# A Fourier-and-gate kernel on one core: the first set of Strassen products reordered, a shared operand left unsplit

## The chip, the cores and the metric

One core of a Trainium2 chip. The metric is the device time of one execution in microseconds; the time of a kernel is the median of several runs. The engines are TensorE (PE), VectorE (DVE), ScalarE (ACT), GpSimd (POOL) and SyncE (SP); SP and POOL issue the transfers, each from a queue of its own, in order.

## The reference

With S = 2048 rows, D = 640 columns and F = 1536 hidden units, all in float32:

```
xn = layernorm(x)                              # rows of 640
a  = xn @ dft_hid_re.T ;  b = xn @ dft_hid_im.T
s  = dft_seq_re @ a - dft_seq_im @ b           # over the 2048 rows
f  = (silu(xn @ w_gate) * (xn @ w_up)) @ w_down
out = x + s * silu(f)
```

The kernel takes the sequence transform first (the DFT matrix over rows times xn, `seq`), then the hidden transform (`hid`), then the gate and up products (`gate_up`) and the down product (`down`).

## The kernel before, in words

**Products.** A float32 product is made of three matmuls in a rounded format: each operand is split into a high part (ScalarE copies it rounded, L192) and a low part (VectorE subtracts, L197 or L199), and `mm3` (L213 to L215) takes high*high, high*low and low*high. A matmul is 128x128 by 128x512.

**Strassen.** `seq(k)` runs four times (two halves of the output rows j, real and imaginary ri). Each time a 1024-row by 2048-column quarter pair of the DFT matrix is cut in four blocks a11, a12, a21, a22 and multiplied by xn's blocks with seven products p1 to p7 over the first 512 columns of xn. The last 128 columns need no Strassen: they are "direct" products that ride beside others into bank 6 or 7, d1 and d2 being xn's upper and lower rows of those columns. D1 = d1*a11 + d2*a12 rides beside p1 and p2. D2 = d1*a21 + d2*a22 is made by a phase of its own, "d" (operand a21 against d1), and by the first pass of p4 (a22 against d2). A product runs in four groups g = 0 to 3, each of two tiles kk of 128 rows; a group of p5 before is 12 matmuls (two banks), a group of d 6, a group of p1 or p2 with its direct product 18.

**The order of the work** is made by a planner. `Plan` counts TensorE's steps at MM = 0.226 us a matmul; each other operation is given a lead (`prod`: so many us ahead of the step that needs it) or an `after` (`post`), and all are sorted by the resulting time and issued in that order, each engine's queue in order. `LEAD` (L541) holds the leads of the first set by hand. Tiles live in two arenas, "hl" for split operands (95 KB a partition) and "raw" for all else (111 KB); `place` and `fit` choose each tile's place from the times at which it is used, so a later tile can have to wait for an earlier one's last reader.

**The opening** (`opening`, first set) runs p1 of k = 0 and, beside it, p1 of k = 1 (it has the same right operand), in eight steps kk of two parts: part 0 into banks b2 and 6, part 1 into banks b1 and b3[0]. Step 0 is unsplit and counts 24 x 0.226 = 5.42 us, each later one 18 matmuls, and the whole 33.90 us. Behind it, sums of part 1 are copied out by two evictions (L241, planned 1 us after the end) to s1 and d1, kept for k = 1. SP loads x tiles 0 to 7 and a11 of both parts for it, x tiles of 128 rows by L412 and parts of the DFT matrix by L684, L686 and L575.

**Behind the opening**, for k = 0: phase d: `d(g)` loads a21 (R[g], 512 KB), splits it, and lets POOL add a22 onto R[g] in memory (`accumulate`, L580, a transfer that adds; it must wait until the split has read R[g]). Then p5, whose left operand is R[g] = a21 + a22, in the order of groups 0, 2, 3, 1, into banks b3; when a group's operand is split, POOL adds a11 onto R[g] for p6. Then p2 with a12, for which x tiles 8 to 15 are loaded (8 and 9 by SP, the others by POOL), normalized (small steps on POOL, L442 to L449) and split. Then p6, p3, p7, p4. For k = 1 to 3 the order is p1 (not for k = 1), d, p2, p5, p6, p3, p7, p4. Sums of xn's blocks that p5, p6, p4 need (nt1, t2, nt4) are made once by `new` (L478) in "raw" and kept through all four sets.

**Gate, up and down.** `gate_up(j)` takes 12 steps f of 54 matmuls; `gate_weights` loads 640 KB (L911) 16 us ahead of each step, forms sums on VectorE (L918) and splits them in four parts. The down product is a Strassen product of the same kind (`strassen`): p1, d, p2, p5 and so on. Its weight operands are prepared during the gate steps of j = 0 by `down_operands`, one name of `d_names` at a time in two slots of each of ten steps f, stored to DRAM split (L533) and loaded from there (L1021).

Of the kernel before, what the change touches and what calls it, by code (L numbers as in the profile page):

```python
# [7 lines left out]
F32 = mybir.dt.float32  # L8
# [14 lines left out]
MM = 0.226  # L23
HL_KB, RAW_KB = 95, 111


class Plan:
# [10 lines left out]
    def buf(self, name, arena, n):  # L38

        for key in ((name, "h"), (name, "l")) if arena == "hl" else (name,):  # L40
            self.size[key] = (arena, n if arena == "raw" else n // 2)
        return name
# [95 lines left out]
def tile_fnet_swiglu(  # L138
# [23 lines left out]
    hl_arena = one.tile([P, HL_KB * 256], F32R, name="hl")  # L162
    raw_arena = one.tile([P, RAW_KB * 256], F32, name="raw")
    ps = psum.tile([P, 8, TC], F32, name="ps")
    mv = one.tile([P, NS, 2], F32, name="mv")
# [7 lines left out]
    def raw(name, a=0, n=None):  # L173
        o = where[name]
        return raw_arena[:, o + a:o + (pl.size[name][1] if n is None else a + n)]

    def hl(name, i, a=0, n=None):

        key = name, "hl"[i]
        o = where[key]  # L180
        return hl_arena[:, o + a:o + (pl.size[key][1] if n is None else a + n)]

# [68 lines left out]
    def strassen(tag, groups, get, top, dop, result, end=False):  # L251
# [72 lines left out]

        def a21(g):
            X[g] = get(21, g)
            return operand("d", g, X[g])

        def a12(g):
# [3 lines left out]
        def s_1(g):  # L333
            V[g] = get(22, g)
            name = pl.buf(("W", tag, g), "raw", n[g])
            W[g] = (name, 0, (name, 0))
            (xn_, xa, xk), (vn, va, vk) = X[g], V[g]
            pl.prod(12, lambda: nc.vector.tensor_tensor(
                raw(name), raw(xn_, xa, n[g]), raw(vn, va, n[g]), op=ALU.add), [xk, vk], [(name, 0)])
            return operand("p5", g, W[g])  # L340
# [15 lines left out]
        evict(s1, b2)  # L356
        phase("d", None, a21, (2, 1))
        phase("p2", b1, a12, (1, 2))
        result(11, b1, s1, ALU.subtract)
        result("d1", (dbank[1],), None, None)  # L360
        phase("p5", b3, s_1)
        n5 = copies("n5")
# [14 lines left out]
        if not end:  # L377
            run("p4", ops["p4"], None, None, None, (2, 2))
            result("d2", (dbank[2],), None, None)
            run("p4", ops["p4"], b2, w, wk)  # L380
            result(21, b2, None, None)
            return
        dw, dkeys = dop(2)

# [82 lines left out]
    def right(p, g, lead):  # L467


        def quad(h, c, w=256):  # L470
            k = 8 * h + 4 * g
            return (lambda a=0, n=4: xn_tiles(k + a, n, 256 * c, w)), [(xn, i, c) for i in range(k, k + 4)]

        def new(what, a, b, op):
            if (what, g) not in sums:
                name = pl.buf((what, g), "raw", 1024)
                view = lambda a=0, n=4: raw(name).rearrange("p (a b) -> p a b", b=256)[:, a:a + n]
                pl.prod(lead, lambda: nc.vector.tensor_tensor(view(), a[0](), b[0](), op=op), [*a[1], *b[1]], [(name, 0)])  # L478
                sums[what, g] = view, [(name, 0)]
            return sums[what, g]  # L480

        if p == "p1":
            return quad(0, 0)
        if p == "p2":
            return quad(1, 0)
        if p == "p3":
            return quad(1, 1)
        if p == "p5":
            return new("nt1", quad(0, 0), quad(0, 1), ALU.subtract)
        if p == "p6":  # L490
            return new("t2", quad(1, 1), sums["nt1", g], ALU.add)
        if p == "p4":
            return new("nt4", quad(1, 0), sums["t2", g], ALU.subtract)
        if p == "p7":
            a, b = quad(0, 1), quad(1, 1)
            if ("nt3", g) not in sums:
                pl.prod(lead, lambda: nc.vector.tensor_tensor(a[0](), a[0](), b[0](), op=ALU.subtract), b[1], a[1])
                sums["nt3", g] = a
            return a
        return quad(int(p[1]) - 1, 2, P)  # L500


    d_names = ("p1", "p2", "d1", "d2", "p3", "p5", "p6", "p7", "p4")
    d_dram = {(p, g): dram.tile([P, 768 if p[0] == "d" else 1536], F32, name=f"d_{p}_{g}") for g in range(2) for p in d_names}

    def down_operands():

        for g in range(2):
# [10 lines left out]
            for p in d_names:  # L519
                b11, b12, b21, b22 = (quad(*q) for q in ((0, 0), (0, 1), (1, 0), (1, 1)))  # L520
                made = {"p5": (b11, b12, ALU.subtract), "p6": (b11, b22, ALU.add),
                        "p7": (b12, b22, ALU.subtract), "p4": (b21, b11, ALU.subtract)}
                if p in made:
# [22 lines left out]

# [8 lines left out]
    def seq(k):  # L555
# [54 lines left out]

        def run(*parts, order=None):

# [4 lines left out]
            start = pl.now  # L617
            for i, g in order or [(0, g) for g in range(4)]:
                p, left, banks, direct = parts[i]
                rights = ([p] if banks else []) + ([f"d{direct[1]}"] if direct else [])  # L620
                per = 3 * (len(banks) + (direct is not None))
                at = pl.now
                s = left(g)
                for kk in (2 * g, 2 * g + 1):
                    pl.now = at + kk % 2 * per * MM
                    for r in rights:
                        few = 4 if not fresh or r not in ("p1", "d1", "p2", "d2") else 2 if g > 2 or r[1] == "2" else 1
                        if (r, kk) not in top:
                            right_operand(r, kk // few, few)
                pl.now = at + 2 * per * MM  # L630
                todo.append((p, g, banks, direct, rights, s))
# [29 lines left out]
        def copy(what, b):  # L661
            name = pl.buf((what, k), "raw", 2 * TC)
            evict(name, b, after=3)
            return name
# [3 lines left out]
        def opening():  # L668
# [42 lines left out]
            for kk in range(8):  # L711
                for i, banks, db in part:
                    c = left[i, kk // 2]
# [13 lines left out]
            ahead["d1"] = pl.buf(("d1", 1), "raw", TC)  # L727
            evict(ahead["s1"], b1, after=1)
            evict(ahead["d1"], (b3[0],), after=1)

# [3 lines left out]

        def p5(g):
            s = operand("p5", g, R[g])
            if fresh:
                accumulate(R[g], 11, g, LEAD["p5", g][1] - 0.1)
            return s

        def d(g):
            R[g] = load(21, g, 26 if fresh else 18)
            s = operand("d", g, R[g])
            accumulate(R[g], 22, g, LEAD["d"][1] - 0.1 if fresh else 7.5)
            return s

        def p2(g):
            if fresh:
                for kk in (8 + 2 * g, 9 + 2 * g):
                    load_x(kk, (32, 27.5, 25.4, 29.4)[g], nc.gpsimd if g else nc.sync)  # L750
                layer_norm(8 + 2 * g, 2, *LEAD["xn", 4 + g], nc.gpsimd)
            return operand("p2", g, load(12, g, 11 if fresh else 17))

# [9 lines left out]
        def p3(g):  # L763
            add(R[g], load(12, g, 17), 12)
            return operand("p3", g, R[g])
# [10 lines left out]
        s1 = ahead["s1"] if shared else copy("s1", b2)  # L776
        run(("d", d, (), (2, 1)))
        if not fresh:
            product_2()
        run(("p5", p5, b3, None), order=((0, 0), (0, 2), (0, 3), (0, 1)) if fresh else None)  # L780
        n5 = copy("n5", b3)
# [15 lines left out]
        def p4(g):  # L797
            last.append(operand("p4", g, load(22, g, 17)))
            return last[-1]

        run(("p4", p4, (), (2, 2)))
        result("d2", (dbank[2],), None, None)
# [104 lines left out]
    def gate_weights(j, f):  # L907
        names = [pl.buf(("W", j, f, i), "hl", 2 * n) for i, n in enumerate((512, 640, 640, 384))]
        w = pl.buf(("wraw", j, f), "raw", 1280)
# [22 lines left out]
    def gate_up(j):  # L932
# [5 lines left out]
        for f in range(NF):  # L938
# [44 lines left out]
            pl.post(lambda g1=g1: nc.scalar.activation(raw(g1), raw(g1), AF.Silu, scale=-1.0), [(g1, 0)], [(g1, 0)])  # L983
            if j == 0 and f and f != NF - 1:
                next(spare, None)
# [22 lines left out]
            tail.append(last)  # L1008
            if j == 0 and f and f != NF - 1:
                next(spare, None)  # L1010
# [71 lines left out]

    where.update(pl.place({"hl": HL_KB * 256, "raw": RAW_KB * 256}))

# [4 lines left out]
    started = False  # L1089
    for t, _, fn, names, _ in pl.ops:  # L1090
        if t >= 0 and not started:
# [43 lines left out]
```

## Time and profile before

| | us |
|---|---|
| median of 3 runs | 992.88 (992.24 to 993.19) |
| the profiled execution, its time | 993.8 |
| the profiled execution, its span (first to last instruction) | 991.7 |
| TensorE busy | 979.3 |
| VectorE busy | 717.2 |
| ScalarE busy | 497.8 |
| POOL busy | 106.4 |
| mean granted clock of TensorE | 0.995 of full |

The span leaves out 2.1 us of the profiled execution's time. All times inside the run are microseconds from the span's start. TensorE's matmuls overlap, so its duration per matmul (0.39 us in the timeline) is longer than the distance of two starts (0.227 us); the distance is what adds up.

### The profile page before, as it was taken

The page shows a single profiled execution, that of the slowest core. Times are in us where ns is not written, and L with a number is a line of the kernel's source. Part 1 is how long each engine was busy: PE and PEld are TensorE (multiplying, and loading weights), DVE is VectorE, ACT ScalarE, POOL GpSimd, SP SyncE. Part 2 cuts the span into 40 slices and gives each one's busy share as a digit, 9 for nine tenths or more (in the row PEclk, how much of TensorE's full clock was granted, in tenths as well). Part 3 has the DMA queues.
Part 4 walks back from the last instruction along what each step waited for, and adds up shares of the span by engine and source line. Part 5 has one row for each costly group of instructions (what it writes and reads, how often), then busy time and mean ns, then how long its engine had stood idle before and what let it go on. Part 6 is the DMA issues. An engine that isn't in the chain of part 4 may idle for free.

```text
span 991.7 us, 11754 instructions
## 1 busy us (share of the span) xinstructions
PE 979.3 (99%) x4300; PEld 804.7 (81%) x4300; DVE 717.2 (72%) x942; ACT 497.8 (50%) x716; POOL 106.4 (11%) x175
## 2 busy tenths in 40 slices
PE   9989999999999999999999999999999999999998
PEld 5778888788888888888888888888888888888886
DVE  6889867965875595377678787687568666666685
ACT  5585652755455554424655555444334544445342
POOL 0380111011101010000111110000010100000000
PEclk9989999999999999999999999999999999999999
DMA  9788687575757493842645344679860211105683
GB/s 337 208 210 227 223 217 180 171 237 135 180 191 222 108 264 116 288 163 107 250 191 181 138 165 164 211 264 354 293 230 28 89 45 53 54 27 191 219 290 127
DMA packets 72185, 182.18 MB, mean 184 GB/s; under 512 B 6528, under 2 KB 22144, under 8 KB 72128
## 3 DMA queue, kind: packets, MB, share of 16 engines
q1 hardware_dynamic: 57792, 127.81, 38.0%
q0 software_dynamic: 14336, 53.63, 19.6%
q8 instruction: 33, 0.54, 0.2%
q14 instruction: 24, 0.20, 0.1%
HBM read 147.85 MB, written 33.57 MB: 183 GB/s over the span
## 4 chain that ended last, share of the span: by engine, by line
PE 91%; DMA 3%; DVE 2%; ACT 2%; issue 1%; SPq 0%; POOL 0%; DVEq 0%; ACTq 0%
PE ps L214 30%; PE ps L213 30%; PE ps L215 30%; DMA raw<-in_cs 3%; DVE hl L197 1%; ACT hl L192 1%; DMA p_dram<-raw 1%; ACT raw L454 0%; DVE raw L583 0%; DVE bst L421 0%; ACT raw L241 0%; POOL raw L580 0%; DVE raw L246 0%; SPq L686 0%; SPq L412 0%
## 5 line engine op out<-in xcount | busy, mean ns | idle before, releaser
L213 PE MATMUL ps<-hl 128*128 128x512 f32 (+1 forms) x1424 | 554.6, 389 | 5.3 <-ACT raw L241 5.3
L214 PE MATMUL ps<-hl 128*128 128x512 f32 (+1 forms) x1424 | 554.0, 389 | 0.1
L215 PE MATMUL ps<-hl 128*128 128x512 f32 (+1 forms) x1424 | 553.6, 389 | 0.0
L192 ACT ACTIVATE hl<-raw 128x1024 fp32r<-128x1024 f32 (+7 forms) x509 | 374.5, 782 | 284.4 <-PE ps L215 54.1
L197 DVE TENSOR_TENSOR hl<-raw,hl 128x1024 fp32r<-128x1024 f32 (+5 forms) x438 | 394.7, 931 | 121.8 <-ACT hl L192 76.9
L213 PEld LDWEIGHTS ps<-hl 128*128 128x128 f32 x1424 | 268.0, 188 | 62.5 <-ACT raw L241 6.1
L214 PEld LDWEIGHTS ps<-hl 128*128 128x128 f32 x1424 | 267.9, 188 | 56.2 <-DVE hl L197 0.7
L215 PEld LDWEIGHTS ps<-hl 128*128 128x128 f32 x1424 | 267.9, 188 | 55.2
L241 ACT ACTIVATE raw<-ps 128x512 f32<-128x512 f32 (+1 forms) x120 | 78.0, 670 | 106.6 <-PE ps L215 80.9
L246 DVE TENSOR_TENSOR raw<-ps,raw 128x512 f32<-128x512 f32 (+1 forms) x93 | 74.6, 803 | 54.1 <-PE ps L215 52.4
L1005 DVE TENSOR_TENSOR raw<-raw 128x512 f32<-128x512 f32 x24 | 16.6, 692 | 50.1 <-ACT raw L1004 50.0
L918 DVE TENSOR_TENSOR raw<-raw 128x256 f32<-128x256 f32 (+1 forms) x96 | 47.7, 518 | 0.0
L580 POOL DMA_DIRECT2D raw<-in_cs x36 | 32.3, 953 | 140.3 <-DVE raw L583 81.0
L199 DVE SCALAR_TENSOR_TENSOR hl<-raw,hl 128x384 fp32r<-128x384 f32 (+4 forms) x71 | 41.2, 580 | 7.3 <-PE ps L215 2.9
L583 DVE TENSOR_TENSOR raw<-raw 128x1024 f32<-128x1024 f32 x28 | 34.1, 1219 | 10.8 <-DMA raw<-in_cs 10.7
L1067 POOL DMA_DIRECT2D out<-raw x10 | 6.7, 671 | 302.1 <-DMA hl<-d_p 175.1
L657 POOL DMA_DIRECT2D p_dram<-raw x24 | 17.5, 772 | 198.1 <-DVE raw L246 163.4
L871 DVE TENSOR_TENSOR raw<-raw 128x1024 f32<-128x1024 f32 (+1 forms) x24 | 23.9, 1040 | 6.8 <-DMA raw<-in_xt 4.7
L983 ACT ACTIVATE raw<-raw 128x512 f32<-128x512 f32 x24 | 15.2, 632 | 22.1 <-DVE raw L246 22.1
L843 POOL DMA_DIRECT2D y_dram<-raw x20 | 10.8, 546 | 132.5 <-ACT raw L241 132.5
L1004 ACT ACTIVATE raw<-ps 128x512 f32<-128x512 f32 x24 | 14.3, 594 | 21.0 <-PE ps L215 21.0
L533 POOL DMA_DIRECT2D d_p<-hl x28 | 15.1, 541 | 79.7 <-ACT hl L192 65.6
(49 smaller groups left out, 191.6 us busy)
## 6 DMA issues: line engine op xcount, KB each, us to landing
raw<-in_cs SPq DMA_DIRECT2D x82, 512.0 KB, 6.1
hl<-d_p SPq DMA_DIRECT2D x56, 384.0 KB, 4.4
raw<-in_cs POOLq DMA_DIRECT2D x36, 512.0 KB, 8.9
raw<-in_wb SPq DMA_DIRECT2D x24, 640.0 KB, 4.5
d_p<-hl POOLq DMA_DIRECT2D x28, 384.0 KB, 2.9
raw<-p_dram SPq DMA_DIRECT2D x8, 1280.0 KB, 11.1
p_dram<-raw POOLq DMA_DIRECT2D x16, 512.0 KB, 7.5
raw<-in_hd SPq DMA_DIRECT2D x20, 320.0 KB, 8.1
```

Source lines behind the costliest of these rows:

```text
L192: nc.scalar.activation(like(hl(dst, 0, a, n)), src(), AF.Copy, scale=1.0 if scale is None else scale)
L197: nc.vector.tensor_tensor(lo, src(), hi, op=ALU.subtract)
L199: nc.vector.scalar_tensor_tensor(lo, src(), scale, hi, op0=ALU.mult, op1=ALU.subtract)
L213: nc.tensor.matmul(o, w(0), m(0), start=first, stop=False, skip_group_check=True)
L214: nc.tensor.matmul(o, w(0), m(1), start=False, stop=False, skip_group_check=True)
L215: nc.tensor.matmul(o, w(1), m(0), start=False, stop=True, skip_group_check=True)
L241: pl.post(lambda: nc.scalar.activation(wide(raw(dst, a, n)), pair(b), AF.Copy), pkeys(b), [(dst, a)], after)
L246: pl.post(lambda: nc.vector.tensor_tensor(wide(raw(dst, a, n)), pair(b), wide(raw(other)), op=op), [*pkeys(b), (other, 0)], [(dst, a)], after)
L580: pl.prod(lead, lambda: nc.gpsimd.dma_start(wide(raw(name)), source(q, g), accum_op=ALU.add), [], [(name, 0), (name, 1)], 8)
L583: pl.prod(lead, lambda: nc.vector.tensor_tensor(raw(dst), raw(dst), raw(src), op=ALU.add), [(src, 0)], [(dst, 0)])
L871: pl.prod(46 - 6 * q - 2 * i - half, lambda i=i, op=op, part=part, rows=rows, nb=nb: nc.vector.tensor_tensor(part(), part(), raw(rows, i * ...
L918: pl.prod(lead, lambda o=o, a=a, b=b, op=op: nc.vector.tensor_tensor(o(), a(), b(), op=op), [(w, 0)], [(c, lead)])
```

## The change

D2 is now d1*(a21 + a22) + d3*a22 with d3 = d2 - d1. The phase d is gone in all sets and in the down product: its direct product rides beside p5 with p5's own operand, and a21 is split nowhere. d3 is one more sum of xn's blocks (`nt5`) and one more name among the down weights, in whose slots now all twelve steps f of the first gate pass take part. In the first set p5 follows straight on the opening, in the order 0 to 3; a21's loads, a22's accumulates and the x tiles 8 to 15 (all on SP now) have earlier leads; the last opening step takes part 1 first, and the two evictions are planned 1.5 and 1 us ahead of its end instead of 1 us behind. The sums (and s1 of the first set) lie in an area "raw2" of 28 KB, which is closed after its last use and opened again as "hl2" for parts 1 to 3 of the gate weights; "hl" falls to 84 KB and "raw" to 94. Some leads of loads grow by 3 us.

```diff
-HL_KB, RAW_KB = 95, 111
+HL_KB, RAW_KB, TURN_KB = 84, 94, 28
...
-        def a21(g):
-            X[g] = get(21, g)
-            return operand("d", g, X[g])
-
         def s_1(g):
-            V[g] = get(22, g)
+            X[g], V[g] = get(21, g), get(22, g)
...
-        phase("d", None, a21, (2, 1))
         phase("p2", b1, a12, (1, 2))
...
-        phase("p5", b3, s_1)
+        phase("p5", b3, s_1, (2, 1))
...
-            run("p4", ops["p4"], None, None, None, (2, 2))
+            run("p4", ops["p4"], None, None, None, (2, 3))
...
-        def new(what, a, b, op):
+        def new(what, a, b, op, w=256):
             if (what, g) not in sums:
-                name = pl.buf((what, g), "raw", 1024)
+                name = pl.buf((what, g), "raw2", 4 * w)
...
+        if p == "d3":
+            return new("nt5", quad(1, 2, P), quad(0, 2, P), ALU.subtract, P)
...
-    d_names = ("p1", "p2", "d1", "d2", "p3", "p5", "p6", "p7", "p4")
+    d_names = ("p1", "p2", "d1", "d2", "d3", "p3", "p5", "p6", "p7", "p4")
...
-            ("p5", 0): (7.7, 6.7), ("p5", 1): (8.4, 7.4), ("p5", 2): (7.2, 6.2), ("p5", 3): (7.4, 6.4), "p2": (8, 6), "d": (8.7, 8.4)}
+            "Tp2": (0, 6, 4), "Td2": (0, 6, 4), "T": (14, 13, 11), "S": (10, 8), "p5": (7.4, 6.4), "p2": (8, 6)}
...
-            name = pl.buf((what, k), "raw", 2 * TC)
+            name = pl.buf((what, k), "raw2" if fresh and what == "s1" else "raw", 2 * TC)
...
-                for i, banks, db in part:
+                for i, banks, db in part if kk < 7 else part[::-1]:
...
-            evict(ahead["s1"], b1, after=1)
-            evict(ahead["d1"], (b3[0],), after=1)
+            evict(ahead["d1"], (b3[0],), after=-1.5)
+            evict(ahead["s1"], b1, after=-1)
...
         def p5(g):
+            R[g] = load(21, g, 33 + 4 * g if fresh else 26)
+            accumulate(R[g], 22, g, 22 + 2 * g if fresh else 18)
             s = operand("p5", g, R[g])
             if fresh:
-                accumulate(R[g], 11, g, LEAD["p5", g][1] - 0.1)
-            return s
-
-        def d(g):
-            R[g] = load(21, g, 26 if fresh else 18)
-            s = operand("d", g, R[g])
-            accumulate(R[g], 22, g, LEAD["d"][1] - 0.1 if fresh else 7.5)
+                accumulate(R[g], 11, g, LEAD["p5"][1] - 0.1)
             return s
...
-                    load_x(kk, (32, 27.5, 25.4, 29.4)[g], nc.gpsimd if g else nc.sync)
+                    load_x(kk, 40 + 2 * g, nc.sync)
...
-            return operand("p2", g, load(12, g, 11 if fresh else 17))
+            return operand("p2", g, load(12, g, 11 if fresh else 20))
...
-        run(("d", d, (), (2, 1)))
         if not fresh:
             product_2()
-        run(("p5", p5, b3, None), order=((0, 0), (0, 2), (0, 3), (0, 1)) if fresh else None)
+        run(("p5", p5, b3, (2, 1)))
...
-        run(("p4", p4, (), (2, 2)))
+        run(("p4", p4, (), (2, 3)))
...
-        names = [pl.buf(("W", j, f, i), "hl", 2 * n) for i, n in enumerate((512, 640, 640, 384))]
+        names = [pl.buf(("W", j, f, i), "hl2" if i else "hl", 2 * n) for i, n in enumerate((512, 640, 640, 384))]
...
-            if j == 0 and f and f != NF - 1:
+            if j == 0:
                 next(spare, None)
...
-    for t, _, fn, names, _ in pl.ops:
+    first = ExitStack()
+    space["raw2"] = first.enter_context(tc.tile_pool(name="sums", bufs=1)).tile([P, TURN_KB * 256], F32, name="raw2")
+    for i, (t, _, fn, names, _) in enumerate(pl.ops):
+        if i == turn:
+            first.close()
+            space["hl2"] = ctx.enter_context(tc.tile_pool(name="parts", bufs=1, reuse_waits="tile")).tile(
+                [P, TURN_KB * 256], F32R, name="hl2")
```

## Rows read from the trace of the kernel before

**Rows 1.** The page: span, busy time of each engine (share of the span, instructions).
```profile
span 991.7 us, 11754 instructions
...
PE 979.3 (99%) x4300; PEld 804.7 (81%) x4300; DVE 717.2 (72%) x942; ACT 497.8 (50%) x716; POOL 106.4 (11%) x175
```

**Rows 2.** TensorE's waits (us, times, longest): whole run, then 100 to 991 us.
```profile
PE ps L213 <- ACT raw L241: 5.3, 2, 5.0
...
PE ps L213 <- ACT raw L241: 0.2, 1, 0.2
```

**Rows 3.** Windows: length, busy of each engine (x instructions), granted clock, DMA share, GB/s.
```profile
12.48:41.10 28.62, 28.62 (x126) 23.18 (x125) 24.58 (x57) 19.40 (x32) 4.38 (x6) 1.00 0.79 289
...
47.20:52.20 5.00, 0.04 (x1) 0.00 (x0) 2.22 (x5) 2.42 (x4) 4.55 (x10) 0.85 1.07 211
52.20:57.55 5.35, 5.26 (x12) 4.12 (x13) 5.28 (x10) 5.35 (x8) 4.51 (x6) 0.50 1.04 332
```

**Rows 4.** TensorE's timeline around the hole: start, duration, what, [idle before].
```profile
46.85 0.39 PE L215 MATMUL ps<-hl 128*128 128x512 f32 x1
52.28 0.79 PE L213 MATMUL ps<-hl 128*128 128x512 f32 x1 [5.05 <-ACT raw L241]
...
57.55 0.40 PE L213 MATMUL ps<-hl 128*128 128x512 f32 x1
```

**Rows 5.** The chain of waits, 36 to 53 us: start, duration, engine and line.
```profile
39.50 10.25 DMA raw<-in_cs
...
49.78 1.06 ACT hl L192
50.83 1.41 ACT raw L241 x2
```

**Rows 6.** POOL's timeline: the first accumulate.
```profile
36.72 1.06 POOL L580 DMA_DIRECT2D raw<-in_cs  x1 [35.39 <-DVE hl L197]
```

**Rows 7.** SP's timeline, 14 to 23 us, and the landing of its first four L575.
```profile
15.30 3.78 SPq L575 DMA_DIRECT2D raw<-in_cs  x4
19.55 1.12 SPq L412 DMA_DIRECT2D raw<-in_x  x2
...
DMA to landing us min/median/max: 8.9/9.3/9.3
```

**Rows 8.** Accumulates (L580), issue to landing: the first one, then all 12 to 100 us.
```profile
DMA to landing us min/median/max: 5.7/5.7/5.7
...
DMA to landing us min/median/max: 5.7/8.9/14.6
```

**Rows 9.** DMA: windows as in rows 3; then 36 to 60 us in 40 slices, share and GB/s.
```profile
24.00:31.00 7.00, 7.00 (x33) 5.79 (x32) 5.69 (x18) 4.67 (x11) 0.00 (x0) 1.00 1.03 402
31.00:36.70 5.70, 5.70 (x27) 4.72 (x26) 4.63 (x8) 5.67 (x10) 0.00 (x0) 1.00 0.14 57
...
DMA  0000929998997999999999999999999999999995
GB/s 0 0 0 0 123 41 218 212 205 220 316 205 247 316 218 218 198 191 218 218 198 198 212 198 218 212 212 212 205 218 381 427 418 418 410 289 205 218 212 96
```

**Rows 10.** Groups by line and shape: the splits (busy us, mean ns, idle before).
```profile
L197 DVE TENSOR_TENSOR hl<-raw,hl 128x1024 fp32r<-128x1024 f32 x186 | 220.4, 1220 | 61.8 <-ACT hl L192 38.6 <-PE ps L214 11.8 <-PE ps L215 11.3
L192 ACT ACTIVATE hl<-raw 128x1024 fp32r<-128x1024 f32 x190 | 191.8, 1052 | 126.7 <-PE ps L214 37.2 <-PE ps L215 34.1 <-DVE raw L885 14.0
...
L197 DVE TENSOR_TENSOR hl<-raw,hl 128x1536 fp32r<-128x1536 f32 x32 | 55.9, 1754 | 16.3 <-ACT hl L192 12.1 <-PE ps L215 2.4 <-PE ps L214 1.1
...
L192 ACT ACTIVATE hl<-raw 128x1536 fp32r<-128x1536 f32 x32 | 46.9, 1485 | 38.1 <-DVE raw L288 20.6 <-issue 7.3 <-PE ps L215 7.2
L197 DVE TENSOR_TENSOR hl<-raw,hl 128x512 fp32r<-128x512 f32 x62 | 42.6, 687 | 21.3 <-ACT hl L192 9.6 <-PE ps L214 8.1 <-PE ps L215 2.0
```

**Rows 11.** Gate weights: their loads (KB each, us to landing) and first sum.
```profile
raw<-in_wb SPq DMA_DIRECT2D x24, 640.0 KB, 4.5
...
L918 DVE TENSOR_TENSOR raw<-raw 128x640 f32<-128x640 f32 x24 | 19.6, 818 | 0.0
```

More of the change, by code (lines that the diff above doesn't have):

```diff
@@ L38, in buf @@
     def buf(self, name, arena, n):
-        for key in ((name, "h"), (name, "l")) if arena == "hl" else (name,):
-            self.size[key] = (arena, n if arena == "raw" else n // 2)
+        split = arena[:2] == "hl"
+        for key in ((name, "h"), (name, "l")) if split else (name,):
+            self.size[key] = (arena, n // 2 if split else n)
         return name
@@ L163, in tile_fnet_swiglu @@
     raw_arena = one.tile([P, RAW_KB * 256], F32, name="raw")
+    space = {"hl": hl_arena, "raw": raw_arena}
     ps = psum.tile([P, 8, TC], F32, name="ps")
@@ L174, in raw @@
         o = where[name]
-        return raw_arena[:, o + a:o + (pl.size[name][1] if n is None else a + n)]
+        arena, size = pl.size[name]
+        return space[arena][:, o + a:o + (size if n is None else a + n)]
     def hl(name, i, a=0, n=None):
@@ L180, in hl @@
         o = where[key]
-        return hl_arena[:, o + a:o + (pl.size[key][1] if n is None else a + n)]
+        arena, size = pl.size[key]
+        return space[arena][:, o + a:o + (size if n is None else a + n)]
     def split(lead, dst, n, src, reads, a=0, scale=None, sub=0, low_lead=None):
@@ L382, in strassen @@
             return
-        dw, dkeys = dop(2)
+        dw, dkeys = dop(3)
         def alone(bank, weights, keys, first, a=0, n=TC):
@@ L472, in quad @@
             return (lambda a=0, n=4: xn_tiles(k + a, n, 256 * c, w)), [(xn, i, c) for i in range(k, k + 4)]
-        def new(what, a, b, op):
+        def new(what, a, b, op, w=256):
             if (what, g) not in sums:
-                name = pl.buf((what, g), "raw", 1024)
-                view = lambda a=0, n=4: raw(name).rearrange("p (a b) -> p a b", b=256)[:, a:a + n]
+                name = pl.buf((what, g), "raw2", 4 * w)
+                view = lambda a=0, n=4: raw(name).rearrange("p (a b) -> p a b", b=w)[:, a:a + n]
                 pl.prod(lead, lambda: nc.vector.tensor_tensor(view(), a[0](), b[0](), op=op), [*a[1], *b[1]], [(name, 0)])
@@ L521, in down_operands @@
                 made = {"p5": (b11, b12, ALU.subtract), "p6": (b11, b22, ALU.add),
-                        "p7": (b12, b22, ALU.subtract), "p4": (b21, b11, ALU.subtract)}
+                        "p7": (b12, b22, ALU.subtract), "p4": (b21, b11, ALU.subtract),
+                        "d3": (quad(1, 2, P), quad(0, 2, P), ALU.subtract)}
                 if p in made:
@@ L609, in tw, with run @@
             return lambda part: hl(name, part, at + e * P, P)
-        def run(*parts, order=None):
+        def run(part):
             todo = []
             start = pl.now
-            for i, g in order or [(0, g) for g in range(4)]:
-                p, left, banks, direct = parts[i]
+            p, left, banks, direct = part
+            for g in range(4):
                 rights = ([p] if banks else []) + ([f"d{direct[1]}"] if direct else [])
@@ L763, in p3 @@
         def p3(g):
-            add(R[g], load(12, g, 17), 12)
+            add(R[g], load(12, g, 20), 12)
             return operand("p3", g, R[g])
@@ L797, in p4 @@
         def p4(g):
-            last.append(operand("p4", g, load(22, g, 17)))
+            last.append(operand("p4", g, load(22, g, 20)))
             return last[-1]
-        run(("p4", p4, (), (2, 2)))
+        run(("p4", p4, (), (2, 3)))
         result("d2", (dbank[2],), None, None)
@@ L1008, in gate_up @@
             tail.append(last)
-            if j == 0 and f and f != NF - 1:
+            if j == 0:
                 next(spare, None)
@@ L1081, in tile_fnet_swiglu @@
         down(j)
-    where.update(pl.place({"hl": HL_KB * 256, "raw": RAW_KB * 256}))
+    where.update(pl.place({"hl": HL_KB * 256, "raw": RAW_KB * 256, "raw2": TURN_KB * 256, "hl2": TURN_KB * 256}))
+    uses = [{pl.size[n if n in pl.size else (n, "h")][0] for n in names if n in pl.size or (n, "h") in pl.size} | {
+        pl.size[n][0] for n in names if n in pl.size} for _, _, _, names, _ in pl.ops]
+    turn = 1 + max(i for i, u in enumerate(uses) if "raw2" in u)
+    assert not any("hl2" in u for u in uses[:turn])
     nc.gpsimd.memset(sm[:, 5, :8], EPS)
```

1 row of the table LEAD is left out of this document.

## The prediction

> **What bounds the kernel now.** I began with the page's table of busy time [rows 1]: TensorE is busy 979.3 of 991.7 us, so only what happens while it is idle or slow can change the time. The waits of TensorE come next [rows 2]: over the whole run it waited 5.3 us in two places for ScalarE's evictions at L241, and behind 100 us only 0.2 us of that is left. So there is one hole, of 5.0 us. The timeline of TensorE places it [rows 4]: a matmul starts at 46.85, the next at 52.28. The windows around it show the second half of the price [rows 3]: in the opening TensorE ran 126 matmuls in 28.62 us at full granted clock, 0.227 us each; behind the hole, from 52.20 to 57.55, the granted clock is 0.50 (1.2 GHz instead of 2.4) and 12 matmuls take the time of 23. From the start at 46.85 to the start at 57.55 there are 13 matmuls: 10.70 us where 13 x 0.227 = 2.95 are due. **The hole costs 7.75 us in all**: some 5.2 of standing and some 2.55 of slow clock.
>
> Why it is there, by the chain of waits [rows 5]: an accumulate landed at 49.75 after 10.25 us, ScalarE split that operand from 49.78, and only then, from 50.83, ran the evictions for which TensorE waited. Those evictions had their sums since the end of the opening, 6 us earlier; they stood behind the split in ScalarE's queue. By the plan's numbers that is so: the second p5 group (g = 2) is due at 33.90 + 5.42 + 2.71 - 7.2 = 34.83, the evictions at 33.90 + 1 = 34.90. And the accumulate was late because POOL could start the first of them only at 36.72, after 35.39 us of waiting for a VectorE split [rows 6]: a22 is added in place onto a21, and a21's own split had to be read out first. The loads of a21 had been issued at 15.30 and took 8.9 to 9.3 us [rows 7], so the first lay there from about 24.6. Between 31.0 and 36.7 the DMA engines moved 57 GB/s, against 402 before [rows 9]: they stood almost still, waiting for that split.
>
> **The change, part by part.** TensorE's work does not shrink. d1*a21 + d2*a22 becomes d1*(a21+a22) + (d2-d1)*a22: 24 matmuls of d move into p5 and 24 stay in p4, the same number of the same shape. So no term of TensorE's busy time goes.
>
> *Splits.* Gone are 16 splits of 128x1024 in the four sets and 4 of 128x1536 in the down products: ScalarE 16 x 1.052 + 4 x 1.485 = 22.8 us, VectorE 16 x 1.220 + 4 x 1.754 = 26.5 us [rows 10]. Added are 8 splits of 128x512 for d3, 8 x 0.687 = 5.5 us on VectorE and about as much on ScalarE, two sums nt5, by the same row about 1.4 us, and for the down weights two sums, two splits, four stores and eight loads of small tiles, some microseconds over the whole run. All of it lies on engines that TensorE does not wait for behind 100 us [rows 2]: I price it at nothing. If the cover were gone, the two extra steps beside the gate products would cost what VectorE lacks there; it is 72% busy over the run [rows 1].
>
> *The first set.* Accumulates wait for their own a21 load alone. The first is in at 24.6; an accumulate that finds its queue empty lands 5.7 us after its issue [rows 8], so the first is in by 30.3. With accumulates flowing the engines moved about 212 GB/s [rows 9]: 524 KB take 2.47 us, and if an x load (328 KB, 0.82 us at 402 GB/s) goes between each two, one lands every 3.3 us: about 31, 34.5, 37.7 and 41. Needed: trace time is plan time plus 7.06 (the second opening step is due at 5.42 and began at 12.48 [rows 3]). The opening ends at 41.1, where p5 now begins. Its first operand is due on ScalarE at 33.90 - 7.4 + 7.06 = 33.6, the second at 37.6. Both have their sums. A p5 group now takes 18 x 0.227 = 4.1 us instead of 2.7, so later accumulates have more time.
>
> *The evictions.* p5's bank is now needed at once, where d gave 5.4 us of cover. The last opening step is turned round: the part that fills banks b1 and b3[0] ends 9 x 0.227 = 2.0 us before the other, at 39.1, and the eviction of b3[0] is due at 32.40 in plan time, behind the second operand's split (30.57) and ahead of the third's (34.64). One bank at most takes what the wider evictions take in the chain, 1.41 us for two [rows 5]; done by 40.5, 0.6 us ahead. Above that bound TensorE waits; below, nothing. I take nothing.
>
> *Moved loads.* The x tiles 10 to 15 leave POOL's queue for SP's, where 8 and 9 are already [rows 7]; all eight stand right behind a21's loads. POOL then holds only accumulates and the small layernorm steps; the third accumulate of a11 stands behind the layernorm of x tiles 8 and 9, which waits for those loads. SP holds a12's loads behind them.
>
> *Memory.* The sums and one copy move to 28 KB of their own, later given to gate weights; the split arena falls from 95 to 84 KB and the plain one from 111 to 94. No row prices where a planner puts tiles. A gain is bounded by the 0.2 us of rows 2; a loss, by the pattern below, reaches some 14 us. I take nothing, being nearest to rows 2: TensorE waits nowhere else now, and the set's longest-lived split tile (d2 from p2 to p4) goes.
>
> **The sum.** The profiled execution took 993.8 us, 991.7 of it span, 0.9 above the median of 992.88. 993.8 - 7.75 = 986.05; on the median's scale **985.1 us**.
>
> **Rivals.** *A. p2 starves.* TensorE reaches p2 at 41.1 + 72 x 0.227 = 57.4, against 57.55 + 36 x 0.227 = 65.7 before: 8.3 us sooner, and the x tiles and a12 must be there sooner too. From 24.6 the DMA engines owe, before p2's first operand: three loads of a21 (3.9 us), eight x loads (6.6), a12 (1.3), four accumulates of a22 (9.9) and two of a11 (4.9): 26.6 us, up to 51.2; landing and split (some 4) bring it to 55.5, 2 us ahead. If another two accumulates get in front (4.9), p2 waits 3 us, and with up to 2.55 of slow clock behind it the time is 987 to 990.5. For it: DMA shares of nine tenths and more through nearly all of 38 to 60 us before [rows 9]. Against: 5.7 us of nearly idle DMA [rows 9] are now used. The Trainium skill ("DMA: Bandwidth & Descriptors", Queues, rings and completion order) speaks for it: each DMA engine goes round the queues that have work, a packet at a time, so that accumulates on POOL's queue are not held behind SP's loads but take turns with them. No row here shows the turns themselves; by that rule the sum would be this rival's.
>
> *B. The same head-of-line wait, one operand later.* If the second accumulate lands not at 34.5 but with the longest time seen, 14.6 us [rows 8], after an issue at 26.5, it is there at 41.1; split and eviction then end near 42.9, and p5 waits 1.8 us: 986.5 to 988.
>
> *C. Slower: the gate weights in 94 KB.* A gate step is 54 matmuls, 12.24 us. Its weights take 4.5 us to land, and a sum 0.82 [rows 11], its splits some 0.8. A load that finds room by 12.24 - 4.5 - 0.8 = 6.9 us into the step before costs nothing. If the planner puts the next weights where the present sums lie, which are read until plan time +7 and its split, 7.6, each step waits some 0.6 us: 24 x 0.6 = 14 us, 999. It decides where half the steps are hit. Against: these loads are issued 16 us ahead, and the split arena there grows (84 + 28 against 95).
>
> *D. No change.* The stall only moves: whatever ended last at 49.8 was DMA work, and the same bytes are still to be moved. If all of it came back at p2, 992.9. The idle 5.7 us speak against it.
>
> **How the numbers follow.** A measurement of this kernel can tell about 0.2% (2 us) from no change. Forecast 0.60 (984.4 to 986.2, the 0.2 us of rows 2 and half a microsecond of run difference below, 1 above); A 0.17; B 0.08; D 0.06; C 0.09. Range 984.4 to 990.5, which holds the forecast, A and B; C's 999 and D are what it leaves out. Faster: forecast, A and B, 0.85; same, D, 0.06; slower, C, 0.09.
>
> **What would show it.** Right: no idle TensorE at the end of the opening and a granted clock of 1.00 from there to 60 us; the first POOL accumulate near 24.6 with no VectorE wait ahead; no DMA dip between 31 and 36.7; matmuls still 4300; p2 starting near 57.4. A wrong forecast shows as a TensorE wait: near 57 for SP's loads (A), near 41 for L241 behind L192 (B), between 470 and 920 for L192, L197 or L199 fed by the weights (C). If the hole goes and the time does not, C or a wait that I have not named took it.

## The result and the profile after

The changed kernel takes 994.47 us (median of 20 runs, 993.7 to 995.2) against 992.89 for the kernel before (20 runs): a ratio of 1.0015, 95% interval 1.0009 to 1.0022. The forecast was 985.1. The hole it was made for is gone all the same; the time was lost again in another place, and for the most part not by a wait.

The page of the changed kernel, span and busy times:

```profile
span 991.9 us, 11749 instructions
...
PE 984.0 (99%) x4300; PEld 803.7 (81%) x4300; DVE 699.8 (71%) x936; ACT 483.3 (49%) x706; POOL 105.9 (11%) x173
```

TensorE has as many instructions as in [rows 1], but is busy 4.7 us longer. Windows of the changed kernel (columns as in [rows 3]), over the old hole and over the second gate pass:

```profile
41.10:47.20 6.10, 6.10 (x29) 5.05 (x28) 5.05 (x12) 4.37 (x6) 3.87 (x8) 1.00 1.05 283
47.20:52.20 5.00, 5.00 (x24) 4.14 (x23) 3.95 (x11) 2.89 (x4) 4.02 (x10) 1.00 1.05 294
52.20:57.55 5.35, 5.35 (x25) 4.45 (x24) 5.28 (x11) 5.35 (x9) 4.37 (x11) 1.00 1.04 245
...
770.00:920.00 150.00, 150.00 (x645) 121.11 (x645) 91.85 (x180) 66.71 (x134) 0.41 (x1) 1.00 0.25 82
```

The same window of the second gate pass in the kernel before:

```profile
770.00:920.00 150.00, 150.00 (x663) 124.20 (x663) 95.04 (x182) 74.03 (x144) 2.15 (x4) 1.00 0.22 76
```

Where [rows 3] count 13 matmuls in the two windows from 47.2 to 57.55, at a granted clock of 0.85 and 0.50, there are now 49 at 1.00 (a matmul that lies across an edge counts in both windows; by their starts there are 12 and 45). But in the gate pass, busy to the last tenth at a granted clock of 1.00 in both kernels, 150 us hold 645 matmuls instead of 663: 18 x 0.227 = 4.1 us lost in 150 us without one wait. The groups of TensorE by shape say which matmuls (count | busy us, mean ns); the program's names keep two tiles apart, and "hl,hl" are those that take their weights from the new area hl2 and their moving operand from hl:

```profile
L217 PE MATMUL ps<-hl 128*128 128x512 f32 x1076 | 419.4, 390 | 0.0
...
L217 PE MATMUL ps<-hl,hl 128*128 128x512 f32 x336 | 133.3, 397 | 1.1 <-ACT raw L245 1.1
```

Each of the three lines of `mm3` has 336 of them, 1008 in all, 7 ns longer on average. By the distances of starts, they take 0.234 us instead of 0.227. From 400 us to the end, waits left out, all matmuls together took some 8.1 us more than as many in the kernel before; 1008 x 7.4 ns = 7.5 of it are these. The last column shows the other new cost, a wait of 1.1 us at 484 us. So the balance is -7.75 (the hole) -0.2 (the small wait of [rows 2]) +8.1 +1.1 = +1.3; the medians differ by +1.6. The two traces differ by less, 991.9 us of span against 991.7. By the distances of starts the changed kernel gains 0.9 us between 100 and 200 us, not only the 0.2 of idle time; and the traced run of the kernel before lies 0.9 above its median, that of the changed kernel 0.6 below its own.

The part that was forecast came out. POOL's timeline of the changed kernel (start, duration, [idle before]):

```profile
24.36 1.06 POOL L581 DMA_DIRECT2D raw<-in_cs  x1 [23.04 <-DMA raw<-in_cs]
25.63 0.89 POOL L581 DMA_DIRECT2D raw<-in_cs  x1 [0.21 <-issue]
```

The first accumulate starts at 24.36 with the landing of its a21 load, 12.4 us earlier than in [rows 6].

### The profile page after: what moved, and what is told of

It reads as the page before. It is cut to its first block, busy times and chain, and to the rows that moved or that the text cites. A ratio compares the mean times of both kernels' runs of the same rounds, so it can differ in the third digit from the quotient of the medians.

```text
span 991.9 us, 11749 instructions
## 1 busy us (share of the span) xinstructions
PE 984.0 (99%) x4300; PEld 803.7 (81%) x4300; DVE 699.8 (71%) x936; ACT 483.3 (49%) x706; POOL 105.9 (11%) x173
## 4 chain that ended last, share of the span: by engine, by line
PE 98%; ACT 1%; issue 1%; DVE 0%; POOL 0%; POOLq 0%
PE ps L217 32%; PE ps L218 32%; PE ps L219 32%; PE ps L228 1%; PE ps L460 1%; ACT raw L245 0%; ACT hl L196 0%; ACT L1088 0%; DVE raw L250 0%; POOL y_dram L839 0%; DVE hl L203 0%; DVE hl L201 0%; DVE raw L1059 0%; DVE raw L1061 0%; DVE raw L914 0%
## 5 line engine op out<-in xcount | busy, mean ns | idle before, releaser
L196 ACT ACTIVATE hl<-raw 128x1024 fp32r<-128x1024 f32 (+7 forms) x499 | 360.4, 765 | 284.7 <-PE ps L219 74.8
L201 DVE TENSOR_TENSOR hl<-raw,hl 128x1024 fp32r<-128x1024 f32 (+5 forms) x428 | 375.7, 907 | 136.3 <-ACT hl L196 72.1
L217 PE MATMUL ps<-hl 128*128 128x512 f32 x1088 | 422.8, 389 | 0.0
L218 PE MATMUL ps<-hl 128*128 128x512 f32 x1088 | 422.5, 388 | 0.0
L219 PE MATMUL ps<-hl 128*128 128x512 f32 x1088 | 422.0, 388 | 0.0
L217 PEld LDWEIGHTS ps<-hl 128*128 128x128 f32 x1088 | 204.3, 188 | 43.0 <-ACT hl L196 0.4
L218 PEld LDWEIGHTS ps<-hl 128*128 128x128 f32 x1088 | 204.3, 188 | 42.6 <-DVE hl L201 0.3
L219 PEld LDWEIGHTS ps<-hl 128*128 128x128 f32 x1088 | 204.3, 188 | 42.3 <-DVE hl L203 0.2
L217 PE MATMUL ps<-hl,hl 128*128 128x512 f32 x336 | 133.3, 397 | 1.1 <-ACT raw L245 1.1
L218 PE MATMUL ps<-hl,hl 128*128 128x512 f32 x336 | 133.1, 396 | 0.0
L219 PE MATMUL ps<-hl,hl 128*128 128x512 f32 x336 | 133.1, 396 | 0.0
L250 DVE TENSOR_TENSOR raw<-ps,raw 128x512 f32<-128x512 f32 (+1 forms) x93 | 74.7, 804 | 62.9 <-PE ps L219 61.6
L217 PEld LDWEIGHTS ps<-hl,hl 128*128 128x128 f32 x336 | 63.3, 188 | 16.9 <-ACT raw L245 1.5
L219 PEld LDWEIGHTS ps<-hl,hl 128*128 128x128 f32 x336 | 63.3, 188 | 15.5
L218 PEld LDWEIGHTS ps<-hl,hl 128*128 128x128 f32 x336 | 63.2, 188 | 15.2
```

Source lines behind the costliest of these rows:

```text
L196: nc.scalar.activation(like(hl(dst, 0, a, n)), src(), AF.Copy, scale=1.0 if scale is None else scale)
L201: nc.vector.tensor_tensor(lo, src(), hi, op=ALU.subtract)
L217: nc.tensor.matmul(o, w(0), m(0), start=first, stop=False, skip_group_check=True)
L218: nc.tensor.matmul(o, w(0), m(1), start=False, stop=False, skip_group_check=True)
L219: nc.tensor.matmul(o, w(1), m(0), start=False, stop=True, skip_group_check=True)
L250: pl.post(lambda: nc.vector.tensor_tensor(wide(raw(dst, a, n)), pair(b), wide(raw(other)), op=op), [*pkeys(b), (other, 0)], [(dst, a)], after)
```

## Experiments

All but the last (b1) are the changed kernel with the edits shown. Times were taken in four sessions; the kernel before, run beside them, took 992.85 us (e1 to e4), 992.35 (f1, f2, b1), 992.29 (g1, g2; one run) and 992.67 (h1 to h3). The kernels e3, f2, g1, g2, h2 and h3 were run once each, so that their times have no interval; the counts of matmuls come from one trace of each kernel. The table sums up what the next sections argue. "Start" is the byte of a partition at which the built program puts an area; within the areas all split tiles lie at multiples of 512 bytes. "In 150 us" are the matmuls in the window 770 to 920.

| kernel | hl2 starts | hl starts | difference mod 256 | in 150 us | time, us |
|---|---|---|---|---|---|
| before | (one arena) | 16512 | 0 | 663 | 992.9 |
| changed | 200672 | 16512 | 96 | 645 | 994.47 |
| e1_area_64 | 200640 | 16512 | 64 | 648 | 993.20 |
| e2_area_32 | 200608 | 16512 | 32 | 649 | 992.65 |
| e3_all_32 | 200640 | 16544 | 32 | 649 | 992.21 |
| e4_area_64_old_slots | 200640 | 16512 | 64 | 648 | 992.11 |
| f1_area_low | 16512 | 45184 | 0 | 664 | 986.01 |
| f2_split_arena_high | 16512 | 141440 | 0 | 663 | 985.89 |
| g1_split_mid_area_top | 200672 | 112768 | 96 | 646 | 993.45 |
| g2_area_above_split | 104416 | 16512 | 96 | 645 | 993.47 |
| h1_top_in_step_128 | 200576 | 16512 | 0 | 664 | 985.97 |
| h2_low_out_of_step | 16512 | 45216 | 224 | 648 | 992.30 |
| h3_top_in_step_256 | 200448 | 16512 | 128 | 651 | 991.27 |

### First: the start address alone?

The area begins 32 bytes past a multiple of 64, the arena hl at a multiple. Three edits of a few bytes, z being the tile of the warming matmuls that lies below the area:

```diff
 e1:  z = one.tile([P, 496], BF16, name="z")
 e2:  z = one.tile([P, 480], BF16, name="z")
 e3:  z = one.tile([P, 480], BF16, name="z")
+e3:  pad = one.tile([P, 8], F32, name="pad")
      hl_arena = one.tile([P, HL_KB * 256], F32R, name="hl")
```

> The changed kernel with the idle tile z cut from 512 to 496 columns, so that the shared 28 KB area begins 32 bytes earlier in each partition, at a multiple of 64 instead of 32 past one; the 16 warming matmuls run 496 columns. Nothing else moves. Theory (start address of the weights): in the changed kernel the 1008 matmuls whose weights lie in that area start every 0.234 us, all others every 0.226 to 0.227; here all start every 0.227, the 8.1 us that the stretch from 400 us to the end lost come back, and the time is 986.4 (985.5 to 987). Rival (a second area costs, wherever it begins: two tiles in one matmul, or memory at the top): 0.234 stays, 994.4. Rival (the gate steps' other traffic, contention with VectorE and ScalarE writing the same area): 0.234 stays, 994.4.

> The control: z cut to 480 columns, so the area begins 64 bytes earlier than in the changed kernel, still 32 past a multiple of 64. Theory (start address): 0.234 us for the 1008 matmuls as in the changed kernel, 994.4 (993.6 to 995.2). Rivals (a shorter z or any move of the area helps): as the run with 496 columns.

> z of 480 columns and a tile of 32 bytes ahead of the split arena: the split arena and the plain one now begin 32 past a multiple of 64, the 28 KB area at a multiple of 64: the reverse of the changed kernel. Theory (start address of the weights alone counts): the gate matmuls with weights in the area at 0.227, all other split products at 0.234; about 3230 of them x 8 ns = 26 us more than the aligned kernel, some 1012. If the moving operand's start counts as well, the gate matmuls too are slow or the others slower than 0.234, 1016 or more. Rivals (a second area costs; contention): the gate matmuls keep 0.234 and the rest 0.227, about 994.4.

All three theories missed. The rivals' time, 994.4, was missed as well, but the slow pace in the gate steps stayed as they had it: 0.233 us by the distances of starts. e1 took 993.20 us (ratio to before 1.0004, interval 0.9995 to 1.0014), e2 992.65 (0.9999, 0.9990 to 1.0008), e3 992.21. The control e2 ended 1.8 us below the changed kernel; some 1 us of that is its slightly better pace (0.233 for 0.234), the rest is not settled. Moving the area to a multiple of 64 gave back hardly any of the 8 us, and in e3, where hl begins 32 past a multiple of 64, the 3228 matmuls that live in hl alone kept their speed while the gate matmuls, with aligned weights, kept their slowness:

```profile
L218 PE MATMUL ps<-hl 128*128 128x512 f32 x1076 | 419.1, 389 | 0.0
...
L218 PE MATMUL ps<-hl,hl 128*128 128x512 f32 x336 | 133.0, 396 | 1.0 <-ACT raw L246 1.0
```

(groups of TensorE of e3, where the line numbers are one higher). The start modulo 64, of the weights or of the moving operand alone, is not the cause. That left the rivals: two areas, the place at the top, contention.

### The slots of the down weights

```diff
-            if j == 0:
+            if j == 0 and f and f != NF - 1:
                 next(spare, None)
```

> The run with 496 columns and, beside it, the down weights' slots back to the steps 1 to 10 of the first gate pass (20 slots for 20 pieces). Theory: the wait of 1.1 us for an eviction near 484 us in the changed kernel is the first gate step made fuller by two of those pieces; here it goes, 985.2 (984.4 to 986). Rival (it comes from where the planner puts tiles in the smaller arenas): it stays near 484, and the time is as with 496 columns alone, 986.4.

992.11 us (0.9994, 0.9985 to 1.0003), 1.1 less than e1, and the wait, 1.5 us in e1, is gone; the expected level was missed with e1's. In the changed kernel the timeline of ScalarE shows why (start, duration, [idle before]):

```profile
477.49 1.24 ACT L196 ACTIVATE hl<-raw 128x768 fp32r<-128x768 f32 x2
483.42 1.15 ACT L196 ACTIVATE hl<-raw 128x768 fp32r<-128x768 f32 x2 [4.69 <-issue]
484.48 1.07 ACT L245 ACTIVATE raw<-ps 128x512 f32<-128x512 f32 x2
```

The 128x768 splits are pieces of the down weights, now in the first gate step too. ScalarE stood idle for 4.69 us ahead of one of them, until 483.42 (for what, the profile does not name), and the eviction that TensorE needed stood behind it in the queue. There are 20 pieces and the old condition has 20 slots, so the new slots were not needed.

### Then: the place

```diff
 f1, f2:
-    one = ctx.enter_context(tc.tile_pool(name="one", bufs=1))
+    one = ctx.enter_context(tc.tile_pool(name="one", bufs=1, side="right"))
 f2, beside it:
+    raw_arena = one.tile([P, RAW_KB * 256], F32, name="raw")
     hl_arena = one.tile([P, HL_KB * 256], F32R, name="hl")
-    raw_arena = one.tile([P, RAW_KB * 256], F32, name="raw")
```

and e4's slots, z at 512.

> The changed kernel with the old slots for the down weights and the 28 KB area at the bottom of each partition (from byte 16512) instead of the top (from 200672); the other arenas lie above it, the plan within them is the same, z has its 512 columns. The start address mod 64 did not matter, so what is left is where the area lies or that it is a second area. Theory (place in memory: weights read from the top, in the changed kernel above 200 KB, load later): the 1008 matmuls go from 0.233 to 0.227, 7 us less than the run with the old slots and the area at the top (992.1): 985 (984.4 to 986). Rival (two tiles in one matmul, or an area opened late): 0.233 stays, 992. Rival (contention with the writers of the gate weights, which write the same tiles at the same times): 0.233 stays, 992.

> The same, but the split arena is put at the top (bytes 141440 to 227456) and the plain arena below it: a scan. By the plan's places 1632 matmuls have weights that begin at 176 KB or higher, 970 at 192 KB or higher, 417 at 208 KB or higher; the moving operands lie there in 2440, 1616 and 743. Theory (place of the weights): the matmuls with weights above some bound take 0.233 and all others 0.227; with the bound at 192 KB some 970 x 6.6 ns = 6.4 us more than the run with the area low, 991.4. If the moving operand's place counts too, those 1616 are slower as well and the time is above 995. Rivals (second area, contention): no dependence on the address, the gate matmuls at 0.233, as the run with the area low.

f1 came out as the theory of the place had it: 986.01 us (0.9935, 0.9921 to 0.9948), and 664 matmuls in 150 us:

```profile
770.00:920.00 150.00, 150.00 (x664) 124.20 (x663) 95.57 (x177) 69.24 (x133) 0.00 (x0) 1.00 0.29 95
```

f1 rules out both rivals: the same two tiles in one matmul, opened at the same moment, written by the same engines at the same times, and no slowness. But f2, meant as a scan of that theory, contradicted it: 985.89 where 991.4 was expected. With hl at 141440 to 227456, 970 matmuls have weights above 192 KB by the plan's places, and the time leaves no room for their being slow. Two runs on the pair of places followed:

```diff
 g1:  raw_arena ahead of hl_arena, both in "one" (left side), area on top
 g2:  raw_arena in a pool of its own, side="right"; area directly above hl and the small tiles
```

> The area at the top again (from byte 200672) as in the changed kernel, with the old slots; the plain arena at the bottom (16512 to 112768) and the split arena in the middle (112768 to 198784). With the area low no address of weights was slow, up to 227 KB; slow is so far only the pair of weights at 200 KB and above with moving operands below 102 KB. Theory A (halves: weights at or above byte 131072 with a moving operand below it): 700 matmuls are such pairs here, some in the gate steps and some in other products; these take 0.233, all others 0.227, and the time is 986 + 700 x 6.6 ns = 990.6. Theory B (distance: weights more than some 98 KB above the moving operand): 31 such pairs, all else 0.227, 986.2. Theory C (the area's own place at the top, whatever the moving operand): the 1008 gate matmuls at 0.233, 992.5.

> The area directly above the split arena and the small tiles (104416 to 133088), the plain arena at the top (133088 to 229344): weights above the moving operands as in the changed kernel, but near. Theory A (halves): only 36 pairs cross byte 131072, 0.227 nearly throughout, 986.2. Theory B (distance over 98 KB): 31 pairs, 986.2. Rival (weights in an area that lies above the moving operands' arena, at any distance): the 1008 gate matmuls at 0.233, 992.5. Theory C: 0.227, 986.

Both were slow, 993.45 and 993.47: g1 as theory C had it, g2 as the rival had it, and no theory of places had both. What the two share with the changed kernel is a number that none of the theories had looked at: the difference of the two starts, 87904 in both, is 96 modulo 128, as in the changed kernel. In f1 and f2 it is 0.

### Last: weights and moving operand in step

```diff
 h1:  z = one.tile([P, 464], BF16, name="z")      (area at the top, old slots)
 h3:  z = one.tile([P, 400], BF16, name="z")      (area at the top, old slots)
 h2:  z = one.tile([P, 496], BF16, name="z")      (f1, arenas 32 bytes higher)
```

> All runs so far fit one rule, the relative start: the area's start minus the split arena's start, modulo 128 bytes, was 96 (the changed kernel and the two runs with the old slots and other orders), 64, 32, 32, 64 where the gate matmuls were slow, and 0 in the two runs with the area low, where they were fast. (Within the arenas all tiles lie at multiples of 512 bytes.) Here the area is at the top as in the changed kernel, with the old slots, and z has 464 columns, so that the difference is 184064: 0 modulo 128, 256 modulo 512. Theory (weights and moving operand must start in step, modulo 128 or 256): 0.227 for the 1008 matmuls, 985.5 (984.8 to 986.5). Rivals: the place at the top with the other arenas below (any): 0.233, 992; a period of 512 or more: 0.233, 992.

> The run with the area low and z of 496 columns, by which the other arenas begin 32 bytes higher: area at 16512, split arena at 45216, 32 out of step; nothing else differs from the run with the area low. Theory (relative start): 0.233 comes back for the 1008 matmuls, 992 to 993. Rival (the place: an area below the others is fast): 0.227, 986.

> As the run with z of 464 columns, but with 400: the difference of the starts is 183936, 0 modulo 128 and 128 modulo 256. If the period is 128: 0.227, about 985.5. If it is 256: 0.233, 992 (the run with 464 being fast).

h1 took 985.97 us (0.9927, 0.9914 to 0.9941): the area at the top as in the changed kernel, 96 bytes lower, and the cost is gone. Groups of TensorE of h1:

```profile
L217 PE MATMUL ps<-hl 128*128 128x512 f32 x1076 | 419.0, 389 | 0.0
...
L217 PE MATMUL ps<-hl,hl 128*128 128x512 f32 x336 | 131.1, 390 | 0.7 <-DVE raw L250 0.6
```

h2 is f1 with hl 32 bytes higher and the area at the same byte: slow again, 992.30, 648 in 150 us:

```profile
770.00:920.00 150.00, 150.00 (x648) 121.09 (x647) 92.67 (x178) 67.11 (x132) 0.00 (x0) 1.00 0.26 82
```

So the weights' own address does not decide, but its distance to the moving operand's. h3, 128 out of step modulo 256, is slow too, 991.27 (651). h1's difference is 256 modulo 512, so a period of 256 bytes fits every row of the table: 0 modulo 256 is 0.227 us a matmul, anything else measured (32, 64, 96, 128, 224) 0.232 to 0.234. In this size of matmul the price is 5.5 to 7.5 ns each; at 96 it is 7.4 ns, and 1008 of them make the 7.5 us that g1 and g2 take more than h1. Other differences, and matmuls of other shapes and types, were not measured. Why the relative start matters is not shown by these runs; only that the pace goes by it.

### The hole itself

```diff
-            evict(ahead["s1"], b1, after=1)
-            evict(ahead["d1"], (b3[0],), after=1)
+            evict(ahead["s1"], b1, after=0)
+            evict(ahead["d1"], (b3[0],), after=0)
```

in the kernel before, nothing else.

> The kernel before with one edit: the two evictions behind the opening are planned at its end instead of 1 us behind it, so they stand ahead of the second p5 operand's split in ScalarE's queue. Theory (the hole is a head-of-line wait of the evictions, and the accumulates' lateness a second cause behind it): p5's first group starts at the end of d, near 47.1, and TensorE then waits near 49.8 for the second operand, split by about 52.1: a hole of 2 to 2.5 us instead of 5.2, with or without slow clock behind it; 987.5 to 990.5. Rival (the late accumulates alone make the hole): p5 still starts at 52.3, 992.9. Rival (the queue order alone makes it): no hole, 985.2.

989.81 us (0.9973, 0.9963 to 0.9983), inside the theory's range; both rivals miss. TensorE's timeline of this kernel:

```profile
50.15 0.39 PE L215 MATMUL ps<-hl 128*128 128x512 f32 x1
50.67 0.51 PE L213 MATMUL ps<-hl 128*128 128x512 f32 x1
51.93 0.50 PE L214 MATMUL ps<-hl 128*128 128x512 f32 x1 [0.76 <-DVE hl L197]
53.06 0.50 PE L215 MATMUL ps<-hl 128*128 128x512 f32 x1 [0.64 <-DVE hl L197]
53.41 0.40 PE L213 MATMUL ps<-hl 128*128 128x512 f32 x1
```

p5 starts with d's end now; the second group then waits for the low parts of its operand, which VectorE could make only after the accumulate had landed. In the chain of waits of b1 (start, duration, what):

```profile
39.17 10.36 DMA raw<-in_cs
...
50.65 2.36 DVE hl L197 x2
```

From 50.15 to 53.41 there are 4 matmuls, 3.26 us where 0.91 are due: 2.35 us, and no slow clock behind it in this execution (windows, columns as in [rows 3]):

```profile
49.90:52.50 2.60, 1.65 (x5) 0.56 (x3) 1.85 (x2) 2.09 (x3) 2.35 (x5) 1.00 1.03 205
52.50:57.50 5.00, 4.11 (x17) 3.05 (x18) 4.93 (x10) 4.94 (x7) 4.19 (x6) 1.00 1.04 341
```

Some 1.1 us more go in two short waits at 55.5 and 74 us. So the queue order made a part of the hole and the late accumulate another; how large each is, the runs do not settle. In the traces b1's last matmul comes 4.6 us earlier than that of the kernel before, but by the medians of runs taken side by side (989.81 and 992.35) the one edit of two numbers gains 2.5 us, where the changed first set with its operands in step (h1) gains 6.7. Nor is it shown that the slow clock is gone from every execution: in three of b1's eight runs the mean granted clock is 0.997, as in many runs of the kernel before (0.995 to 0.998), and in the other five it is 0.999 to 1.000.

## Why the prediction failed, point by point

- **The hole, -7.75 us: right.** It is gone with its slow clock [rows 3, 4]: between 45 and 60 us the trace of the changed kernel gains 7.8 us on that of the kernel before. The kernel in step gains 6.7 us in all (h1 against its runs of before, 992.67). b1 bears out the mechanism, evictions behind a split in ScalarE's queue and that split behind an accumulate, but not how much either makes.
- **The step that failed: "I take nothing, being nearest to rows 2", for the new area in memory, and with it that TensorE's work stays as it was, "the same number of the same shape".** The count held, 4300, but not the price of one. I had priced the new area by waits alone and bounded its loss by what a planner can do with places. The runs showed a cost per matmul instead: 1008 matmuls, whose weights start out of step with their moving operand, at 0.234 us instead of 0.227, 7.5 us by themselves and some 8.1 for all matmuls from 400 us on. No wait, idle time or clock shows it.
- **The extra steps beside the gate products, "I price it at nothing": wrong by 1.1 us.** I put them on engines with time to spare on average; in the first gate step the eviction that TensorE needed stood in ScalarE's queue behind one of their splits, which itself waited (e4 against e1).
- **Evictions of p5's bank in time: right.** The eviction of one bank started at 39.67 and took 0.60 us; its sums were due at 39.1, and 41.1 was the limit. So Rival B's wait near 41 us did not come.
- **Rival A (p2 starves): did not happen,** though its mechanism is there. In the changed kernel the x loads took longest to land behind the accumulates (answer on the line of x loads, L411):

```profile
DMA to landing us min/median/max: 9.3/15.3/20.4
```

against 8.9 to 9.3 for the loads of [rows 7]. The first of the eight, issued at 19.4 ahead of the accumulates, took 9.3 us, the last, issued at 27.9, 20.4. The rule of the Trainium skill ("DMA: Bandwidth & Descriptors", Queues, rings and completion order) is that each DMA engine takes turns between the queues that have work. The trace agrees with it but does not single it out, as each x load also stood behind those before it in SP's own queue. TensorE never waited for these loads: the margin that I had estimated at 2 us was enough.
- **Rival C had the right stretch and the wrong cause.** No weight load was late: no wait of TensorE in the gate steps but the one at 484. **Rival D's** time, 992.9, is the nearest, but nothing moved to p2.
- What was left out of the rivals is a change in the matmul's own pace. The list of what would show the forecast wrong named waits only; the sign was the mean duration of one group and the count of matmuls in a window.
- The kernel in step ends at 986.0 instead of 985.1. On the scale of the traced runs the sum is close: it gave 986.05, and h1's traced run took 986.2. In that trace 0.9 us more is gained between 100 and 200 us, and some 1.2 is lost again to waits in the gate steps, 0.6 of it idle time for VectorE (L250). What the runs do not bear out is the 0.9 us that I then took off to come to the median's scale: the traced run of the kernel before lay that far above its median, but h1's only 0.2 above its own. Whether those 0.9 us lay in the hole, no run shows.

## What to carry to other kernels

Where a change puts an operand of a matmul into another tile or area, keep the starts of weights and moving operand a multiple of 256 bytes apart, or check the mean of that group before and after: in these matmuls of 512 columns it cost 2.5 to 3.3% of their time, and no view of waits shows it. A kernel that is busy throughout can still lose time, so compare the matmuls in equal windows, not only idle time. And an eviction that frees a bank is to be issued ahead of any operand that still waits for a transfer.

## What the runs showed of the hardware that was not expected

The pace of a 128x128 by 128x512 matmul in the rounded float32 format depends on the start of its weights relative to that of its moving operand, modulo 256 bytes: 0.227 us in step; 0.232 (128 out of step) to 0.234 (96) otherwise. Where the two are in step, the absolute start, 16512 or 16544 for hl (e3), changes nothing, nor does the place, from byte 16512 to 227456 of a partition (f1, f2). And in the traced run of b1 a stretch of 3.3 us in which TensorE ran only 4 matmuls left the granted clock at 1.00, where the 5.2 us of the hole were followed by half of it [rows 3].
